# Attention and two mixture-of-experts layers in fp32: how the bias groups, the reciprocal sums and the V tails are handled in the attention part

## The chip, the core and the metric

The kernel runs on one core of one Trainium2 chip. The metric is the device time of one execution in microseconds (us). Before the change three runs gave 1418.03, 1415.32 and 1415.49 us, median 1415.49 us.

## The reference

Three stages follow each other; all arithmetic is fp32.

```python
def _attn_ref(q, k, v, w1, b1, w2):                 # B, H, S, D = 2, 8, 576, 64; 32 hidden values
    scores = 1.0 / np.sqrt(D) * np.matmul(q, k.transpose(0, 1, 3, 2))
    psi_rel = np.log1p(np.abs(pos[:, None] - pos[None, :]))
    psi_i = np.log1p(np.maximum(pos[:, None], 1.0))
    h = np.maximum((psi_rel / psi_i)[..., None] @ w1 + b1, 0.0)
    scores = scores + (h @ w2).transpose(2, 0, 1)[None]          # the bias, one map per head
    attn = np.exp(scores - np.max(scores, axis=-1, keepdims=True))
    return np.matmul(attn / (attn.sum(-1, keepdims=True) + 1e-09), v)
def _moe_ref(x, domain_probs, w1, w2):              # 1152 rows of 512, E = 4, F = 1024
    for e in range(E): out += p[:, e:e+1] * (np.maximum(x @ w1[e], 0.0) @ w2[e])
def _moe2_ref(x, w_gate, w1, w2):                   # E = 8; P from exp of logits, 8 Sinkhorn rounds
    for e in range(E): out += P[:, e:e+1] * (np.maximum(x @ w1[e], 0.0) @ w2[e])
```

## The kernel before, in words

The program is written in the order in which each engine works; nothing reorders it. `attention` comes first, `Moe.run` after it. TensorE is called PE here, VectorE DVE, ScalarE ACT, GpSimd POOL; SP issues all DMAs, in order.

**Bias.** The bias depends on the distance of two positions and on the row, so the kernel makes it in 36 groups of 16 rows. For a group four tiles of hidden values are made (`emit_hid`, L267: `tensor_scalar` on DVE or Relu on ACT), PE multiplies them with `w2` (`emit_bias_mm`, L278), ACT scales the product twice, forwards and reversed, into one of three staging rows (`emit_bias_out`, L298, two ACTIVATE at L313), and SP writes the row to DRAM (`bd`, L316). `load_bias` (L243) reads it back, shifted, as the tile `bt` that the scores need. Hidden values live in six places of `hids`; the product uses one bank `bps` where it has at most 512 columns, and otherwise one of the two `sc` buffers that the scores use. `groups(1)` emits one group, `hids(k)` makes k hidden tiles.

**Start.** The first FIRST = 8 groups are made at once (L476 to L491), with one `hids(2)` before and one after each, the first K and Q tiles being prepared between them (`prep_k`, `prep_q`). Then come the first two `load_bias`, which must wait for the eighth write. The other 28 groups are made inside the loop over units.

**Units.** A unit is a tile of 128 rows of queries for a pair of heads and one batch (in the four units of row tile 4, both batches with 64 rows each); there are 36, numbered 0 to 35 here, in the order row tile 0, 4, 1, 2, 3. Units 8 to 11 are row tile 4. Iteration k of the loop at L500 holds, in this order: scores of unit k (`emit_S`, PE L333), at its end on PE the tail of unit k-2 (`emit_tail`: one transpose, L379, and the two sums' reciprocals turned into rows by two 64-column matmuls with the identity, L382); the minimum of the negated scores with the bias added (`emit_max`, DVE L351, two instructions), the reciprocal of unit k-1's sums (L373, DVE); two exponentials on ACT (L364) with the copy of the first four transposed blocks between them (`emit_evac(k-2, 0)`); eight transposes of unit k-2 on PE (L396); one group (two in iterations 5, 8 and 12, with `hids(4)` between); the copy of the second four blocks on ACT; hidden tiles on DVE, with the copy of the tail's block (`emit_evac(k-2, 2)`, L403) on DVE after the first of them; the product with V of unit k-3 (`emit_P`, PE L423) and its scaling (`emit_x`, DVE L433). The tail's block stands in the second `sc` buffer of unit k, so the next unit's scores cannot start before it is copied out. Once all 36 groups are made (from iteration 25), the tail uses the bank `bps` and is copied by ACT, and the second four blocks by DVE.

In iterations 16 to 18 and from 23 on, one part of `piece` (L107 to L122, sums and fp32 splits of the finished rows for the next stage) stands at an iteration's end, a split with its high part on ACT (L99) and its low part on DVE or POOL (L100). From iteration 28 on the first weights are split too.

**V tails.** `load_v` (L196) puts the last 64 rows of V twice into the fifth block of `V`, in partitions 0 to 63 and 64 to 127, and `emit_P` multiplies the fifth block with 64 rows (L420 to L425): the first head in the lower, the second in the upper half.

**Mixture of experts.** From unit 35 on `Moe` takes over. None of its lines change.

## Time and profile before

| what | value |
|---|---|
| median of three runs | 1415.49 us |
| profiled execution, its own time | 1414.98 us |
| its span, first to last instruction | 1413.2 us |
| mean granted TensorE clock | 0.983 |
| PE busy | 1368.4 us (97%) |
| DVE busy | 812.8 us (58%) |
| ACT busy | 500.8 us (35%) |
| POOL busy | 376.1 us (27%) |

Some 1.8 us lie around the span. Attention takes about the first 235 us. The shares are averages over stages: in attention DVE and ACT are much busier than these shares say, and in the mixture of experts PE is. PE's busy time is modelled and says that matmuls are in flight, not that PE is at its peak. In a row of the timeline stand the start, the length, the engine, the line, the operation, the tiles written and read, the shape and the count; in brackets is the idle time of the engine before it and what ended it. "PEld" rows are weight loads, one before each matmul; "SPq" rows are DMA issues. "issue" means that the profile shows nothing that the engine waited for.

### The profile page before, as it was taken

The page shows a single profiled execution, that of the slowest core. Times are in us where ns is not written, and L with a number is a line of the kernel's source. Part 1 is how long each engine was busy: PE and PEld are TensorE (multiplying, and loading weights), DVE is VectorE, ACT ScalarE, POOL GpSimd, SP SyncE. Part 2 cuts the span into 40 slices and gives each one's busy share as a digit, 9 for nine tenths or more (in the row PEclk, how much of TensorE's full clock was granted, in tenths as well). Part 3 has the DMA queues.
Part 4 walks back from the last instruction along what each step waited for, and adds up shares of the span by engine and source line. Part 5 has one row for each costly group of instructions (what it writes and reads, how often), then busy time and mean ns, then how long its engine had stood idle before and what let it go on. Part 6 is the DMA issues. An engine that isn't in the chain of part 4 may idle for free.

```text
span 1413.2 us, 22618 instructions
## 1 busy us (share of the span) xinstructions
PE 1368.4 (97%) x8871; PEld 1177.3 (83%) x8871; DVE 812.8 (58%) x1810; ACT 500.8 (35%) x1184; POOL 376.1 (27%) x351
## 2 busy tenths in 40 slices
PE   6899999899999999999988999999999999999998
PEld 2566677789889898979877899899898898988987
DVE  5776887656355464385487464463553644735643
ACT  4666775324133142244232142241331422413311
POOL 0000122326044062054043062160440521603400
PEclk8899999999999999999999999999999999999999
DMA  6674531102011021011011021020120210200110
GB/s 176 183 181 121 147 104 61 60 30 90 1 60 61 1 90 31 0 55 65 1 60 61 1 83 38 8 89 24 34 87 1 66 54 1 90 31 31 61 38 31
DMA packets 41659, 84.95 MB, mean 60 GB/s; under 512 B 9296, under 2 KB 17232, under 8 KB 41552
## 3 DMA queue, kind: packets, MB, share of 16 engines
q1 hardware_dynamic: 41552, 83.50, 19.5%
q8 instruction: 70, 1.15, 0.3%
q14 instruction: 37, 0.30, 0.1%
HBM read 70.24 MB, written 13.25 MB: 59 GB/s over the span
## 4 chain that ended last, share of the span: by engine, by line
PE 89%; DVE 7%; ACT 2%; issue 1%; DMA 1%; SPq 0%; POOL 0%; DVEq 0%; ACTq 0%; POOLq 0%
PE y L714 41%; PE B L635 16%; PE C L635 10%; PE A L635 10%; PE po L423 3%; PE bps L287 2%; PE sc L333 2%; PE tp L396 2%; ACT s L364 1%; ACT bsts L313 1%; PE sc L382 1%; DVE s L351 1%; ACT at L405 0%; DVE wt L157 0%; PE sc L379 0%
## 5 line engine op out<-in xcount | busy, mean ns | idle before, releaser
L714 PE MATMUL y<-gb,h 128*128 128x512 f32 x2592 | 718.1, 397 | 0.0
L714 PEld LDWEIGHTS y<-gb,h 128*128 128x128 f32 x2592 | 454.4, 190 | 57.4 <-issue 0.2
L162 POOL TENSOR_TENSOR gb<-rawb,gb 128x512 fp32r<-128x512 f32 x94 | 126.3, 1356 | 640.7 <-ACT gb L161 637.0
L643 DVE TENSOR_TENSOR u<-B,s 128x320 f32<-128x320 f32 (+1 forms) x192 | 87.7, 457 | 306.9 <-PE B L635 306.9
L646 ACT ACTIVATE h<-c 128x320 fp32r<-128x320 f32 (+1 forms) x288 | 119.4, 439 | 400.3 <-DVE c L643 399.2
L649 DVE SCALAR_TENSOR_TENSOR h<-c,h 128x320 fp32r<-128x320 f32 (+1 forms) x288 | 169.5, 605 | 48.8 <-ACT h L646 44.0
L643 DVE TENSOR_TENSOR c<-C,u 128x320 f32<-128x320 f32 (+1 forms) x192 | 87.6, 456 | 61.4 <-PE C L635 57.9
L162 POOL TENSOR_TENSOR ga<-rawa,ga 128x512 fp32r<-128x512 f32 x94 | 120.8, 1304 | 4.5 <-ACT ga L161 4.5
L162 POOL TENSOR_TENSOR ga<-wt,ga 128x512 fp32r<-128x512 f32 x94 | 105.3, 1140 | 45.8 <-ACT ga L161 27.4
L657 ACT ACTIVATE s<-A 128x320 f32<-128x320 f32 (+1 forms) x96 | 39.5, 411 | 177.9 <-PE A L635 177.8
L646 ACT ACTIVATE h<-A 128x320 fp32r<-128x320 f32 (+1 forms) x96 | 39.1, 407 | 151.2 <-PE A L635 151.2
L643 DVE TENSOR_TENSOR c<-B,s 128x320 f32<-128x320 f32 (+1 forms) x96 | 43.9, 458 | 81.7 <-PE B L635 80.3
L161 ACT ACTIVATE gb<-rawb 128x512 fp32r<-128x512 f32 x96 | 60.0, 627 | 71.4 <-DMA rawb<-in_w 71.4
L364 ACT ACTIVATE s<-s,stat 128x576 f32<-128x576 f32 x72 | 55.5, 770 | 59.9 <-DVE stat L351 59.9
L635 PE MATMUL A<-x20A,ga 128*128 128x320 f32 x384 | 66.7, 309 | 0.0
L635 PE MATMUL C<-x20S,ga 128*128 128x320 f32 x384 | 66.6, 309 | 0.0
L635 PE MATMUL B<-x20S,ga 128*128 128x320 f32 x384 | 66.5, 308 | 0.0
L635 PEld LDWEIGHTS B<-x20S,ga 128*128 128x128 f32 x384 | 61.4, 188 | 5.7
L635 PEld LDWEIGHTS A<-x20A,ga 128*128 128x128 f32 x384 | 61.4, 188 | 5.6
L635 PEld LDWEIGHTS C<-x20S,ga 128*128 128x128 f32 x384 | 61.3, 188 | 5.7
L351 DVE CUSTOM_DVE_ANT_0 s<-sc,bt 128x576 f32<-128x576 f32 x72 | 51.7, 753 | 15.9 <-DMA bt<-bd 6.4
L287 PE MATMUL bps<-hids,w2n 128*32 128x288 f32 (+17 forms) x352 | 42.1, 523 | 18.6 <-DVE stat L351 8.1
(157 smaller groups left out, 1910.9 us busy)
## 6 DMA issues: line engine op xcount, KB each, us to landing
rawa<-in_w SPq DMA_DIRECT2D x48, 512.0 KB, 4.0
rawb<-in_w SPq DMA_DIRECT2D x48, 512.0 KB, 4.8
bd<-bsts SPq DMA_DIRECT2D x36, 295.5 KB, 3.3
bt<-bd SPq DMA_DIRECT2D x16, 512.0 KB, 4.3
qr<-in_qT SPq DMA_DIRECT2D x40, 64.0 KB, 3.0
kr<-in_kT SPq DMA_DIRECT2D x16, 144.0 KB, 3.2
V<-in_vT SPq DMA_DIRECT2D x4, 512.0 KB, 4.5
bt<-bd SPq DMA_DIRECT2D x8, 256.0 KB, 4.3
```

Of the source, the lines that this page charges most:

```text
L161: sc.activation(out=z(0), in_=src, func=AF.Copy)
L162: lo.tensor_tensor(out=z(1), in0=src, in1=z(0).bitcast(F32), op=ALU.subtract)
L287: pe.matmul(out=o[32 * q:32 * q + 32, j, 0:n], lhsT=w2n, rhs=hid[g, q][:, n * j:n * j + n], start=True, stop=True,)
L351: ve.tensor_tensor_reduce(out=s.rearrange("p (a j) -> p a j", a=2), in0=scps.pop((u, h))[:, :, 0:288], in1=bt[t, p][:, S * h:S * h + S].re ...
L364: sc.activation(out=s, in_=s, func=AF.Exp, scale=-1.0, bias=stat[u][:, h:h + 1], accum_out=stat[u][:, 2 + h:3 + h],)
L423: pe.matmul(out=o[64 * h:64 * h + 64, c0:c0 + n], lhsT=V[p][r, j, col:col + D], rhs=rhs, start=j == 0, stop=j == 4,)
L635: pe.matmul(out=ban[o], lhsT=a, rhs=x[:, z, k, :], start=not more and i == 0, stop=i == 5, skip_group_check=more,)
L643: ve.tensor_tensor(out=t[o], in0=ban[a], in1=t[b], op=ALU.add)
L646: sc.activation(out=h[f][:, 0, half, :], in_=src, func=AF.Relu)
L649: ve.scalar_tensor_tensor(out=h[f][:, 1, half, :], in0=src, scalar=0.0, in1=h[f][:, 0, half, :].bitcast(F32), op0=ALU.max, op1=ALU.subtract,)
L657: sc.activation(out=t["s1"], in_=ban["A"], func=AF.Copy)
L714: pe.matmul(out=self.y[t], lhsT=a, rhs=x, start=g == 0 and f == 0 and i == 0, stop=g == NP - 1 and f == 1 and i == 2,)
```

## The change

1. `load_v` clears the fifth block of V on POOL (`memset`) and then loads, for each head, only that head's columns into its half of the partitions. The fifth product now has 128 rows like the others; the foreign half is multiplied by zeros.
2. `emit_recip2` spreads the two reciprocals of a row over a 128x128 tile `spread` (POOL copy from a broadcast source), and `emit_tail` transposes that tile in one 128-column transpose where two matmuls stood.
3. The copy of the tail's block (`emit_evac(k-2, 2)`) is always on ACT, between the second exponential and the group's scaling.
4. `emit_x` of unit k-4 stands right after `emit_max(k)`; before, that of unit k-3 stood after `emit_P(k-3)`.
5. The first eight groups are made with twelve places for hidden tiles (six more in three tiles of `xa`; `load_k` now turns over four of these tiles, not seven) and three PSUM buffers for the product, hidden tiles are made two groups ahead, and three more groups stand after the first `load_bias`. Iterations 5, 8 and 12 have one group like the others.

```diff
         def load_v(p):
             sy.dma_start(out=V[p][:, 0:4, :], in_=vT[p, 0:512].rearrange("(j p) x -> p j x", p=128))
+            gp.memset(V[p][:, 4, :], 0.0)
             for h in range(2):
-                sy.dma_start(out=V[p][64 * h:64 * h + 64, 4, :], in_=vT[p, 512:576])
+                to, of = (x.rearrange("p (b h d) -> p h b d", b=2, h=2)[:, h] for x in (V[p][:, 4, :], vT[p, 512:576]))
+                sy.dma_start(out=to[64 * h:64 * h + 64], in_=of)
...
+        free = [(i, hids_[:, i * S:i * S + S]) for i in range(6)]
+        taken = {}
+        MORE = 56
...
+            if started == 6:
+                for i in XA[4:]:
+                    x = xa.tile([128, 1280], F32, tag=f"x0{i}", name=f"hid{i}")
+                    free.extend([(6, x[:, 0:S]), (6, x[:, S:2 * S])])
...
-            if nb == 1:
+            if nb == 1 and (made >= FIRST or made % 3 == 1):
                 o = pt.tile([128, 1, 512], F32, tag="bps", name=f"bps{g}", bufs=1)
...
-            ve.reciprocal(stat[u][:, 6:8], stat[u][:, 4:6])
+            st = stat.pop(u)
+            ve.reciprocal(st[:, 6:8], st[:, 4:6])
+            spread[u] = atb.tile([128, 128], F32, tag="spread", name=f"spread{u}", bufs=2)
+            gp.tensor_copy(
+                spread[u].rearrange("p (h d) -> p h d", h=2), st[:, 6:8].unsqueeze(2).to_broadcast([128, 2, D])
+            )
...
             pe.transpose(o[:, 1, :], s[:, 512:640], ident)
-            st = stat.pop(u)
-            for h in range(2):
-                pe.matmul(
-                    out=o[64 * h:64 * h + 64, 0, :], lhsT=st[:, 6 + h:7 + h].to_broadcast([128, 64]),
-                    rhs=ident, start=True, stop=True,
-                )
+            pe.transpose(o[:, 0, :], spread.pop(u), ident)
...
-                        rhs = a[h][:, j, i0:i0 + n] if j < 4 else a[2][r, 1, i0:i0 + n]
+                        rhs = a[h][:, j, i0:i0 + n] if j < 4 else a[2][:, 1, i0:i0 + n]
...
-                            lhsT=V[p][r, j, col:col + D],
+                            lhsT=V[p][:, j, col:col + D],
...
-        hids(4, (1,))
+        hids(8, (1, 5))
         for g in range(FIRST):
-            hids(2, (1,))
             groups(1)
...
+            hids(4, (1,))
...
         load_bias(*tps_[0])
         load_bias(*tps_[1])
         load_k(*kq[5])
+        load_q(*tps_[3])
+        prep_q(*tps_[1])
         prep_k(*kq[2], sc)
-        load_q(*tps_[3])
+        for _ in range(3):
+            groups(1)
+            hids(4)
         prep_k(*kq[3], sc)
...
                     emit_recip2(k - 1)
+                if k >= 4:
+                    emit_x(k - 4)
...
-            late = made == NGR
-            if late and k - 2 < U:
+            if k >= 2 and k - 2 < U:
                 emit_evac(k - 2, 2, sc)
-            ng = 2 if k in (5, 8, 12) else 1
-            for i in range(ng):
-                groups(1)
-                if i < ng - 1:
-                    hids(4)
+            groups(1)
```

The order on ACT in iteration 5 before: `s` are the exponentials, `at` the copies of transposed blocks, `bsts` the scaling of a group (two rows each).

```order
L364 ACTIVATE s_631,stat_630<-s_631,stat_630 128x576
L405 ACTIVATE at_646<-tp_636 128x512
L364 ACTIVATE s_631,stat_630<-s_631,stat_630 128x576
L313 ACTIVATE bsts<-bps_649,cst 128x432
L313 ACTIVATE bsts<-bps_649,cst 128x160
L313 ACTIVATE bsts<-bps_661,cst 128x416
L313 ACTIVATE bsts<-bps_661,cst 128x176
L405 ACTIVATE at_669<-tp_641 128x512
```

The same iteration on ACT in the changed kernel.

```order
L377 ACTIVATE s_678,stat_677<-s_678,stat_677 128x576
L418 ACTIVATE at_696<-tp_686 128x512
L377 ACTIVATE s_678,stat_677<-s_678,stat_677 128x576
L418 ACTIVATE at_699<-sc_662 128x256
L326 ACTIVATE bsts<-bps_701,cst 128x384
L326 ACTIVATE bsts<-bps_701,cst 128x208
L418 ACTIVATE at_709<-tp_691 128x512
```

The copy out of `sc` has come in ahead of the group, and the second group is gone.

DVE between the first eight groups and the minimum of unit 0 (L351) before: the last hidden tiles, then the low parts of two K tiles (`kk`).

```order
L273 TENSOR_SCALAR hids<-T,b1psi 128x464 x3
L273 TENSOR_SCALAR hids<-T,b1psi 128x528 x3
L225 TENSOR_TENSOR kk_289<-kr_137,kk_289 128x576
L225 TENSOR_TENSOR kk_295<-kr_215,kk_295 128x576
L351 ISA s_313,stat_312<-sc_298,bt_280 128x576
```

The same stretch of DVE in the changed kernel (`hidS` are the places in `xa`).

```order
L283 TENSOR_SCALAR hids<-T,b1psi 128x544 x3
L241 CAST qq_296<-qr_134 128x256
L242 TENSOR_TENSOR qq_296<-qr_134,qq_296 128x256
L227 TENSOR_TENSOR kk_299<-kr_137,kk_299 128x576
L283 TENSOR_SCALAR hids<-T,b1psi 128x560 x2
L283 TENSOR_SCALAR hidS_149<-T,b1psi 128x560 x2
L283 TENSOR_SCALAR hidS_150<-T,b1psi 128x576 x2
L283 TENSOR_SCALAR hidS_151<-T,b1psi 128x576 x2
L283 TENSOR_SCALAR hids<-T,b1psi 128x448 x4
L227 TENSOR_TENSOR kk_350<-kr_224,kk_350 128x576
L364 ISA s_368,stat_367<-sc_353,bt_284 128x576
```

Twelve hidden tiles now stand between the first `load_bias` and the first minimum; before, there were none behind the eighth group but the three of the ninth.

PE in iteration 5 behind the scores before (`sc`: the tail, `tp`: the transposes).

```order
L379 MATMUL sc_614<-kept,s_484 128x128
L382 MATMUL sc_614<-kept,stat_483 64x128 x2
L396 MATMUL tp_636<-kept,s_484 128x128 x4
L396 MATMUL tp_641<-kept,s_484 128x128 x4
L287 MATMUL bps_649<-hids,w2n 32x432 x4
L287 MATMUL bps_661<-hids,w2n 32x416 x4
```

The same in the changed kernel.

```order
L397 MATMUL sc_662<-kept,s_535 128x128
L398 MATMUL sc_662<-kept,spread_607 128x128
L409 MATMUL tp_686<-kept,s_535 128x128 x4
L409 MATMUL tp_691<-kept,s_535 128x128 x4
L297 MATMUL bps_701<-hids,w2n 32x384 x4
```

Ten transposes of one shape now follow each other, and one group follows them.

## Rows read from the trace of the kernel before

**Rows 1.** Timeline, DVE: first minimum of units 0, 4, 8, 14, 25 and 35

```profile
33.78 0.76 DVE L351 CUSTOM_DVE_ANT_0 s<-sc,bt 128x576 f32<-128x576 f32 x1 [5.17 <-DMA bt<-bd]
...
57.65 0.75 DVE L351 CUSTOM_DVE_ANT_0 s<-sc,bt 128x576 f32<-128x576 f32 x1
...
79.76 0.76 DVE L351 CUSTOM_DVE_ANT_0 s<-sc,bt 128x576 f32<-128x576 f32 x1 [1.54 <-DMA V<-in_vT]
...
120.01 0.76 DVE L351 CUSTOM_DVE_ANT_0 s<-sc,bt 128x576 f32<-128x576 f32 x1 [0.78 <-PE sc L333]
...
175.40 0.75 DVE L351 CUSTOM_DVE_ANT_0 s<-sc,bt 128x576 f32<-128x576 f32 x1
...
217.75 0.75 DVE L351 CUSTOM_DVE_ANT_0 s<-sc,bt 128x576 f32<-128x576 f32 x1
```

**Rows 2.** Timeline, PE's weight loads in unit 16, to the next unit's scores

```profile
128.73 0.82 PEld L333 LDWEIGHTS sc<-kk,qq 64*128 64x128 f32 x12 [0.17 <-issue]
...
129.72 0.14 PEld L379 LDWEIGHTS sc<-kept,s 128*128 128x128 f32 x1 [0.17 <-issue]
...
130.35 0.85 PEld L396 LDWEIGHTS tp<-kept,s 128*128 128x128 f32 x8 [0.17 <-issue]
...
132.15 0.85 PEld L423 LDWEIGHTS po<-at,V 128*64 128x64 f32 x16 [0.63 <-DVE at L403]
...
133.18 0.19 PEld L423 LDWEIGHTS po<-at,V 64*64 64x64 f32 x4 [0.17 <-issue]
...
133.54 0.82 PEld L333 LDWEIGHTS sc<-kk,qq 64*128 64x128 f32 x12 [0.17 <-issue]
```

**Rows 3.** Timeline, DVE and ACT in unit 16

```profile
129.92 0.76 DVE L351 CUSTOM_DVE_ANT_0 s<-sc,bt 128x576 f32<-128x576 f32 x1 [0.78 <-PE sc L333]
...
130.78 0.78 ACT L364 ACTIVATE s<-s,stat 128x576 f32<-128x576 f32 x1 [1.23 <-DVE stat L351]
...
131.69 0.42 DVE L403 COPY at<-sc 128x256 f32<-128x256 f32 x1
...
132.04 0.77 ACT L364 ACTIVATE s<-s,stat 128x576 f32<-128x576 f32 x1
...
132.80 1.03 ACT L313 ACTIVATE bsts<-bps,cst 128x208 f32<-128x208 f32 x2
```

**Rows 4.** Second group of unit 12 in the timeline; busy time and granted clock after it

```profile
108.44 0.75 PE L287 MATMUL bps<-hids,w2n 128*32 128x320 f32 x8 [2.36 <-ACT bsts L313]
...
109.10:116.00 6.90, 6.90 (x67) 5.58 (x64) 3.45 (x12) 2.41 (x6) 0.00 (x0) 0.51 0.42 109
```

**Rows 5.** Timeline: minimum of unit 9, last bias load for unit 11, its minimum

```profile
87.82 0.76 DVE L351 CUSTOM_DVE_ANT_0 s<-sc,bt 128x576 f32<-128x576 f32 x1
...
95.64 0.60 SPq L254 DMA_DIRECT2D bt<-bd  x1
...
99.40 0.76 DVE L351 CUSTOM_DVE_ANT_0 s<-sc,bt 128x576 f32<-128x576 f32 x1 [1.47 <-PE sc L382]
```

**Rows 6.** Timeline: bias writes, a group's work on ACT and DVE, first eight groups

```profile
8.85 6.90 SPq L316 DMA_DIRECT2D bd<-bsts  x4
...
15.13 2.42 DVE L273 TENSOR_SCALAR hids<-T,b1psi 128x512 f32<-128x512 f32 x6
...
17.14 1.05 ACT L313 ACTIVATE bsts<-bps,cst 128x512 f32<-128x512 f32 x2 [1.34 <-PE bps L287]
...
18.09 0.68 ACT L275 ACTIVATE hids<-T,b1psi 128x480 f32<-128x480 f32 x1
...
23.73 3.41 SPq L316 DMA_DIRECT2D bd<-bsts  x2
```

**Rows 7.** Timeline: a DVE sum alone, and the same beside a POOL instruction

```profile
174.99 0.29 DVE L115 TENSOR_TENSOR rows<-rows,t 128x128 f32<-128x128 f32 x1
...
187.43 0.46 POOL L100 TENSOR_TENSOR x10A<-rows,x10A 128x128 fp32r<-128x128 f32 x1 [0.45 <-ACT x10A L99]
187.50 0.52 DVE L115 TENSOR_TENSOR rows<-rows,t 128x128 f32<-128x128 f32 x1
```

More of the change, by code (lines that the diff above doesn't have):

```diff
@@ L211, in load_k @@
             i = 2 * p + b
-            r = xa.tile([128, 1280], F32, tag=f"x0{XA[i % 7]}", name=f"kr{p}{b}")[:, 0:S]
+            r = xa.tile([128, 1280], F32, tag=f"x0{XA[i % 4]}", name=f"kr{p}{b}")[:, 0:S]
             for h in range(2):
@@ L265, in ranges @@
             return fwd, rev, n, 1 if n <= 512 else 2
+        free = [(i, hids_[:, i * S:i * S + S]) for i in range(6)]
+        taken = {}
+        MORE = 56
         def emit_hid(g, eng, q):
             tt = 4 * g + q
-            i = started % 6 * S
-            x = hids_[:, i:i + S]
+            if started == 6:
+                for i in XA[4:]:
+                    x = xa.tile([128, 1280], F32, tag=f"x0{i}", name=f"hid{i}")
+                    free.extend([(6, x[:, 0:S]), (6, x[:, S:2 * S])])
+            place = free.pop(0)
+            taken[g, q], x = place, place[1]
             n = ranges(g)[2]
@@ L295, in emit_bias_mm @@
                 hid.pop((g, q))
+                place = taken.pop((g, q))
+                if place[0] < 6 or started < MORE:
+                    free.append(place)
             return o
@@ L321, in attention @@
         scps, sm, at_t, po, rc = {}, {}, {}, {}, {}
-        stat = {}
+        stat, spread = {}, {}
         def emit_S(u):
@@ L419, in emit_P @@
                     for h in range(2):
-                        r = slice(0, 128) if j < 4 else slice(64 * h, 64 * h + 64)
                         col = (2 * bb + h) * D
-                        rhs = a[h][:, j, i0:i0 + n] if j < 4 else a[2][r, 1, i0:i0 + n]
+                        rhs = a[h][:, j, i0:i0 + n] if j < 4 else a[2][:, 1, i0:i0 + n]
                         pe.matmul(
                             out=o[64 * h:64 * h + 64, c0:c0 + n],
-                            lhsT=V[p][r, j, col:col + D],
+                            lhsT=V[p][:, j, col:col + D],
                             rhs=rhs,
@@ L463, in hids @@
             for i in range(k):
-                if started < 4 * NGR:
+                if started < 4 * NGR and (free or started == 6):
                     emit_hid(order[started // 4], sc if i in engs else ve, started % 4)
@@ L476, in attention @@
         FIRST = 8
-        hids(4, (1,))
+        hids(8, (1, 5))
         for g in range(FIRST):
-            hids(2, (1,))
             groups(1)
+            if g == 0:
+                prep_q(*tps_[0])
             if g == 1:
-                prep_q(*tps_[0])
                 prep_k(*kq[0], ve)
+            hids(4, (1,))
             if g == 3:
                 load_k(*kq[3])
+            if g == 4:
                 prep_k(*kq[1], ve)
-                prep_q(*tps_[1])
-            if g == 5:
+            if g == 6:
                 load_k(*kq[4])
                 load_q(*tps_[2])
-            hids(2)
         load_bias(*tps_[0])
@@ L510, in attention @@
                     emit_recip2(k - 1)
+                if k >= 4:
+                    emit_x(k - 4)
             elif k == U:
                 emit_recip2(k - 1)
+                emit_x(k - 4)
                 st_sc.close()
@@ L525, in attention @@
                 emit_exp(k, 1)
-            late = made == NGR
-            if late and k - 2 < U:
+            if k >= 2 and k - 2 < U:
                 emit_evac(k - 2, 2, sc)
-            ng = 2 if k in (5, 8, 12) else 1
-            for i in range(ng):
-                groups(1)
-                if i < ng - 1:
-                    hids(4)
+            groups(1)
             if k >= 2 and k - 2 < U:
                 emit_evac(k - 2, 1, sc if made < NGR else ve)
-            hids(1)
-            if k >= 2 and k - 2 < U:
-                if not late:
-                    emit_evac(k - 2, 2, ve)
-            hids(1)
+            hids(2)
             if k < U:
@@ L545, in attention @@
                 emit_P(k - 3)
-                emit_x(k - 3)
+                if k >= U:
+                    emit_x(k - 3)
             if first:
```

## Prediction, made before the changed kernel ran

> **What bounds the kernel now.** I read the start times of the first minimum of chosen units, because every unit passes through that instruction on DVE [rows 1]. They cut the attention part into five stretches: 33.78 us to unit 0, 23.87 to unit 4, 22.11 to unit 8, 40.25 to unit 14, 55.39 to unit 25, and 42.35 to unit 35. What comes after, the mixture of experts, is not touched, and only its start can move.
>
> Then the weight loads of a unit on PE, late in the middle stretch [rows 2]. Unit 16's scores start at 128.73, the next unit's at 133.54: 4.81 us, and between the loads stand only pauses of 0.17 us, always where the tile's form changes, and the time in which the group's matmuls run (the 0.63). So PE sets the pace there. The tail costs 129.72 to 130.35, 0.63 us, for one transpose and two 64-column products, while eight transposes of the same shape take 0.85, or 0.106 each.
>
> Then DVE and ACT of the same unit [rows 3]. The minimum starts 1.19 us after the scores do, the first exponential 0.86 after that, the second 1.26 after the first, and the group's scaling 0.76 later, at 132.80, with 1.03 of work. DVE's copy of the tail's block, which frees the `sc` buffer, started at 131.69, long before the next scores at 133.54. It is not on the path now.
>
> Last, the places with a second group. In iteration 12 PE waits 2.36 us for its one bank until ACT has scaled the first group; behind that wait PE's granted clock is 0.51 for 6.90 us, that is at 1.2 GHz almost throughout, though PE was busy all the time [rows 4].
>
> **The change part by part.** The sum is made against the profiled execution, 1414.98 us; the median of the runs, 1415.49, is 0.5 above it.
>
> *Start.* Eight groups now end when the last bias write is issued: the two writes from 23.73 take 3.41 [rows 6], an issue itself 0.60 [rows 5], so the eighth goes at 26.5; the first went at 8.85 [rows 6]. That is 2.5 us a group. ACT's own work for a group is 1.05 of scaling and 0.68 for one hidden tile, 1.73 us [rows 6]. With twelve places and three PSUM buffers nothing else should hold a group: 8.85 + 7 x 1.73 = 21.0. The K and Q loads queued ahead of the eighth write on SP are moved by nothing and can cost up to one us, so I take 21.9. Everything from that write to the first minimum (26.5 to 33.78, 7.3 us) stays: first minimum at 29.2, **-4.6 us**. Under this cover lie the three groups: on ACT 3 x 1.05, on DVE 12 hidden tiles at 0.40 (six took 2.42 [rows 6]), 4.8 us. They fit into the 7.3 with the preparation of K and Q, but barely. If they don't, the first minimum is late by what sticks out, up to the three groups' own 4.8.
>
> *Units 0 to 3.* Group 8 to 10 no longer share the `sc` buffers with these units, but the K casts stay between ACT and DVE. Nothing gained leaves 23.87; the pace of unit 16 for all four would be 19.2. I take 22.8, near the upper end since those casts stay in order behind the group's scaling: **-1.1**.
>
> *Steady pace.* On PE the second transpose costs 0.106, and one change of form goes: the tail's 0.63 becomes 0.21 (two transposes in the run of ten), -0.42. The V tail in the form of the other four blocks saves one pause of 0.17 and costs nothing, since its four loads take 0.19, as four of the others do (0.85/16 each) [rows 2]. PE's 4.81 becomes 4.22. But the copy of the tail's block now comes after the second exponential on ACT: from scores to that copy's end 1.19 + 0.86 + 1.26 + 0.76, and some 0.4 for the copy itself (0.42 on DVE [rows 3]), then the next scores. That ring is 4.5 us, longer than PE's 4.22. **ACT's queue takes over from PE**, and the pace is 4.5, not 4.22. In row tile 4 the scores are twice as many (about 0.8 more): 5.3.
>
> *Units 4 to 8.* Three at 4.5 and one at 5.3 make 18.8 against 22.11, mostly the second group of iteration 5: **-3.3**.
>
> *Units 8 to 14.* Two second groups and the slow clock lie here [rows 4]. But bias tiles arrive by SP: unit 11's minimum started at 99.40, 3.2 after the issue of its last load at 95.64 had ended, and 11.58 after unit 9's minimum, which is the reader that frees the buffer [rows 5]. SP's queue holds that unit's bias write first (which waits for the group's scaling), then Q, then four loads. Nothing in the change shortens it; the scaling comes 0.27 later behind the moved copy, so two units cost 11.85. Unit 8 to 9 at 5.3, 9 to 11 at 11.85, then three units at about 4.8 (four 64-row products remain in them): 31.5 against 40.25, **-8.7**.
>
> *Units 14 to 25.* Six units have no split part; 4.8 to 5.0 becomes 4.5: -2.6. In the five others DVE's last low part waits for ACT's high part behind exponentials, group and copies, which the change does not shorten, and slack that PE's lateness used to absorb is gone: I give back half. **-1.3**; the bounds are 0 and 11 x 0.59 = -6.5.
>
> *Units 25 to 35.* No groups any more; the same DVE and ACT queue holds split parts in every unit. I take **0**, bounds 0 and -6.5. Moving `emit_x` forward saves DVE a wait there that the split parts use up.
>
> *After unit 35* PE does three more tails and four more V products without pause, -1.9 at most; DVE's weight splits hold half of it: **-1.0**.
>
> *New on POOL and SP.* 36 spread copies: the nearest row is a 128x128 POOL sum of 0.46 [rows 7]. The copy starts after the reciprocal, over 2 us before PE's tail asks for it, so its length is hidden; four memsets hold back only V's tails on SP, which are needed units later. But a DVE sum beside such a POOL instruction took 0.52 instead of 0.29 [rows 7], so each copy may cost DVE some 0.23. DVE has that much to spare in the 4.5; I count nothing, and at most 36 x 0.23 = 8 us. The Trainium skill ("SBUF — State Buffer", Who interferes with whom) says that GpSimd and VectorE share one port pair under an exclusive lock, the loser blocked for the whole instruction. By it up to 0.46 per unit would be lost, 16 us; the row shows half of that for a late overlap.
>
> Sum: -4.6 - 1.1 - 3.3 - 8.7 - 1.3 - 0 - 1.0 = -20.0, **1395.0 us**.
>
> **The rivals.**
> *PE stays the bound.* If the moved copy's ring is shorter than I think, units 14 to 35 gain what PE gains, 0.59 each. For it: PE was busy without a gap there [rows 2]. Against it: the sum of the ring. It would add some 11 us: 1384.
> *The cover is too short.* The three groups stick out of the round trip (+4.8), and ACT's longer ring eats the 2.6 of units 14 to 25 and the 1.0 at the end: 1395 + 8.4, some 1404. For it: the three groups barely fit.
> *DVE blocked by the spread copies, so slower.* Place: DVE's queue behind the reciprocal in every unit. With 20 us gained elsewhere it decides from 20/36 = 0.56 us per copy, if every copy is long and lies on the path; at 0.7 it is 1395 + 25 = 1420. For it: rows 7 show the interference. The skill's lock is this mechanism. Against it: 0.46 is the nearest length.
> *The groups gain nothing.* If the reads of the bias or the K casts set every start and PE's savings are all absorbed, only noise is left: 1415.
>
> **How the numbers follow.** Forecast (1390 to 1400) 0.58, PE stays the bound 0.15, cover too short 0.20, blocked DVE 0.04, nothing gained 0.03. The likeliest case gives 1395.0. The range takes in the forecast, the short cover up to 1405, and of the PE case its slower part, down to 1385. About 0.2%, or 2.8 us, is what a measurement of this kernel can tell from no change; so faster 0.93, within 0.2% 0.03, slower 0.04.
>
> **What would show it.** First minimum near 29 and unit 4's near 52, unit 14's near 102, unit 25's near 156, unit 35's near 198. In units 19 to 22 scores start every 4.5 us, and PE has short waits before them that ACT's copy of `sc` ends. No second group's wait on PE and no slow clock around unit 12. DVE's hidden tiles stay at their length beside the spread copy. Wrong: a first minimum after 31 (the cover), a pace of 4.2 (PE bound), a pace above 4.8 with DVE late (POOL), or bias tiles arriving earlier than 11 us after the buffer's reader.

## The result, and the profile after

Four runs of the changed kernel took 1395.53, 1398.83, 1400.68 and 1400.79 us, median 1399.76; the kernel before took 1415.72 beside them (median of four). The ratio is 0.9878, with a 95% interval from 0.9854 to 0.9902: faster by 1.2%. The forecast was 1395.0 us, with a range from 1385 to 1405. By the medians 16.0 us are gained. The trace is that of the fastest of the four, 1395.53 us; its span is 1393.6 against 1413.2, 19.6 less. The other three have no trace, so where they take their 3 to 5 us more is not shown. PE is busy 1343.9 us (96%), DVE 802.7, ACT 506.7, POOL 389.3.

The first minima of units 0, 4, 8, 14, 25 and 35 in the timeline of DVE:

```profile
28.99 0.76 DVE L364 CUSTOM_DVE_ANT_0 s<-sc,bt 128x576 f32<-128x576 f32 x1 [1.21 <-DMA bt<-bd]
...
53.03 0.75 DVE L364 CUSTOM_DVE_ANT_0 s<-sc,bt 128x576 f32<-128x576 f32 x1
...
71.03 0.76 DVE L364 CUSTOM_DVE_ANT_0 s<-sc,bt 128x576 f32<-128x576 f32 x1 [1.76 <-PE sc L346]
...
103.32 0.76 DVE L364 CUSTOM_DVE_ANT_0 s<-sc,bt 128x576 f32<-128x576 f32 x1 [0.96 <-PE sc L346]
...
155.51 0.74 DVE L364 CUSTOM_DVE_ANT_0 s<-sc,bt 128x576 f32<-128x576 f32 x1
...
198.23 0.76 DVE L364 CUSTOM_DVE_ANT_0 s<-sc,bt 128x576 f32<-128x576 f32 x1
```

Set against [rows 1], unit 35 comes 19.5 us earlier, and the span is 19.6 shorter: all of the gain in this trace is made before unit 35. By stretch it is 4.8 us to unit 0, -0.2 from 0 to 4, 4.1 from 4 to 8, 8.0 from 8 to 14, 3.2 from 14 to 25 and -0.4 from 25 to 35.

PE's weight loads in unit 21 of the changed kernel, a plain unit (with a group, without split parts), and the group's matmuls that run in the 0.76 us where no weights are loaded. Behind them stand the scores' loads of units 21 and 22 in the kernel before:

```profile
135.79 0.83 PEld L346 LDWEIGHTS sc<-kk,qq 64*128 64x128 f32 x12 [0.17 <-issue]
136.78 0.14 PEld L397 LDWEIGHTS sc<-kept,s 128*128 128x128 f32 x1 [0.16 <-issue]
136.83 0.14 PEld L398 LDWEIGHTS sc<-kept,spread 128*128 128x128 f32 x1
136.94 0.91 PEld L409 LDWEIGHTS tp<-kept,s 128*128 128x128 f32 x8
138.02 0.16 PEld L297 LDWEIGHTS bps<-hids,w2n 128*32 128x32 f32 x8 [0.17 <-issue]
138.93 1.07 PEld L435 LDWEIGHTS po<-at,V 128*64 128x64 f32 x20 [0.76 <-DVE rows L445]
140.18 0.83 PEld L346 LDWEIGHTS sc<-kk,qq 64*128 64x128 f32 x12 [0.17 <-issue]
```
```profile
138.02 0.99 PE L297 MATMUL bps<-hids,w2n 128*32 128x464 f32 x8
```
```profile
153.52 0.82 PEld L333 LDWEIGHTS sc<-kk,qq 64*128 64x128 f32 x12 [0.17 <-issue]
...
158.46 0.82 PEld L333 LDWEIGHTS sc<-kk,qq 64*128 64x128 f32 x12 [0.17 <-issue]
```

The rows answer to [rows 2]. The tail is two loads that run on into the eight transposes (136.78 to 136.94, 0.16 us), and the V products are one run of twenty loads with no pause inside. Scores start 4.39 us apart. Nothing but pauses of 0.17 and the group's own matmuls lies between, so **PE still sets the pace here**: the same distance was 4.94 before, and the difference of 0.55 is nearly the whole 0.59 that the two edits were to save on PE.

Around iteration 0 there are waits that the kernel before did not have. SP's queue, ACT and PE in the changed kernel (three cuts of its timeline; the first row is the eighth bias write):

```profile
21.59 0.54 SPq L329 DMA_DIRECT2D bd<-bsts  x1
24.90 0.39 SPq L255 DMA_DIRECT2D bt<-bd  x1
...
26.36 0.47 SPq L256 DMA_DIRECT2D bt<-bd  x1
26.92 1.14 SPq L216 DMA_DIRECT2D kr<-in_kT  x2
28.10 1.24 SPq L232 DMA_DIRECT2D qr<-in_qT  x2
29.44 5.97 SPq L329 DMA_DIRECT2D bd<-bsts  x4
```
```profile
33.82 1.05 ACT L326 ACTIVATE bsts<-bps,cst 128x16 f32<-128x16 f32 x2 [2.40 <-DMA bd<-bsts]
```
```profile
34.92 1.80 PE L346 MATMUL sc<-kk,qq 64*128 64x288 f32 x11 [2.43 <-ACT bsts L326]
```

The bias writes of the three early groups stand in SP's queue behind two bias loads, a K load and a Q load, and go from 29.44 on. Until the first of them has landed there is no free staging row, so the scaling of iteration 0's group waits 2.40 us, and PE, whose scores need the `sc` buffer of that group, waits 2.43. Unit 0 to 1 takes 7.54 us instead of 5.64.

In row tile 4 (units 8 to 11) and at unit 12, DVE waits for bias tiles:

```profile
83.08 0.76 DVE L364 CUSTOM_DVE_ANT_0 s<-sc,bt 128x576 f32<-128x576 f32 x1 [2.70 <-DMA bt<-bd]
...
88.50 0.76 DVE L364 CUSTOM_DVE_ANT_0 s<-sc,bt 128x576 f32<-128x576 f32 x1 [1.76 <-DMA bt<-bd]
...
94.70 0.76 DVE L364 CUSTOM_DVE_ANT_0 s<-sc,bt 128x576 f32<-128x576 f32 x1 [2.51 <-DMA bt<-bd]
```

Where [rows 4] had a clock of 0.51, the changed kernel has full speed in the same units; the longest stretch of its low clock, 1.2 GHz, lies in the first iterations, where PE had waited for the bias (windows: stretch, length, busy time of PE, PEld, DVE, ACT and POOL, granted clock, DMA share, GB/s):

```profile
94.70:103.30 8.60, 6.91 (x127) 5.63 (x123) 6.75 (x22) 7.21 (x18) 1.28 (x4) 1.00 0.58 155
28.90:39.10 10.20, 6.86 (x42) 3.33 (x44) 6.82 (x20) 4.99 (x12) 1.42 (x4) 0.50 0.72 205
```

### The profile page after: what moved, and what is told of

Same layout as the page of the kernel before. It is cut to its first block, busy times and chain, and to the rows that moved or that the text cites. A ratio compares the mean times of both kernels' runs of the same rounds, so it can differ in the third digit from the quotient of the medians.

```text
span 1393.6 us, 22438 instructions
## 1 busy us (share of the span) xinstructions
PE 1343.9 (96%) x8763; PEld 1171.4 (84%) x8763; DVE 802.7 (58%) x1786; ACT 506.7 (36%) x1208; POOL 389.3 (28%) x391
## 4 chain that ended last, share of the span: by engine, by line
PE 83%; DVE 9%; ACT 3%; DMA 2%; issue 1%; SPq 1%; DVEq 0%; ACTq 0%
PE y L726 41%; PE B L647 16%; PE C L647 10%; PE A L647 10%; DVE s L364 2%; PE po L435 2%; PE sc L346 1%; ACT s L377 1%; DMA bt<-bd 1%; PE bps L297 1%; PE tp L409 1%; ACT bsts L326 1%; DMA bd<-bsts 1%; DVE wt L157 0%; ACT at L418 0%
## 5 line engine op out<-in xcount | busy, mean ns | idle before, releaser
L661 DVE SCALAR_TENSOR_TENSOR h<-c,h 128x320 fp32r<-128x320 f32 (+1 forms) x288 | 165.7, 592 | 49.1 <-ACT h L658 43.8
L435 PEld LDWEIGHTS po<-at,V 128*64 128x64 f32 x800 | 39.4, 137 | 33.9 <-DVE rows L445 32.0
L435 PE MATMUL po<-at,V 128*64 128x128 f32 (+1 forms) x800 | 47.7, 267 | 15.6 <-DVE rows L445 15.4
```

The lines of the kernel that those rows point to most:

```text
L435: pe.matmul(out=o[64 * h:64 * h + 64, c0:c0 + n], lhsT=V[p][:, j, col:col + D], rhs=rhs, start=j == 0, stop=j == 4,)
L661: ve.scalar_tensor_tensor(out=h[f][:, 1, half, :], in0=src, scalar=0.0, in1=h[f][:, 0, half, :].bitcast(F32), op0=ALU.max, op1=ALU.subtract,)
```

## The experiments

Theory 1 is that of the prediction: the bias part carries nearly all of the gain (fast start, no second groups), and the time saved on PE by the other edits mostly vanishes in rings through ACT, DVE and SP (a ring is a loop of waits from engine to engine that closes once per unit, so that its sum is the least a unit can take). Theory 2 is that the saved PE time carries it. The measured ratios are to the kernel before on the same chip. Since the clock makes runs differ by a few us, each run is also read by the first minima in its trace, which repeat closely: the changed kernel's second trace is 1.15 us later at unit 0 and agrees with the first within 0.15 us in each stretch after that. Unit 0 to 1 scatters more: 7.09 to 7.71 us in the runs whose edits do not reach it. That a unit "takes" so long means the time from the first minimum of the unit before it to its own. In us:

```
                              unit 0   0-4    4-8    8-14   14-25  25-35   0 to 35
before                         33.78  23.88  22.11  40.25  55.39  42.35   183.98
changed                        28.99  24.04  18.00  32.29  52.19  42.72   169.24
changed, again                 30.14  24.13  18.01  32.15  52.16  42.72   169.17
second groups back             29.70  23.39  21.08  38.95  52.27  42.73   178.42
before + bias part             29.34  23.93  18.73  31.72  55.82  42.35   172.55
two 64-column products         29.45  23.77  19.08  32.16  55.11  42.76   172.88
V tails of 64 rows             29.84  24.55  18.32  33.01  53.21  43.61   172.70
tail's copy on DVE             30.02  23.65  17.68  31.34  51.49  42.69   166.85
output product last            29.52  23.98  18.04  33.94  52.53  41.01   169.50
output product first           29.70  23.97  18.02  32.16  53.31  42.40   169.86
bias loads early               29.49  23.60  18.00  28.85  52.21  42.72   165.38
bias writes early              29.32  22.89  18.01  34.33  52.17  42.72   170.12
three edits combined           29.44  22.10  17.68  28.17  51.48  42.70   162.13
and output product last        29.49  22.40  17.47  28.08  51.45  40.98   160.38
```

**The changed kernel again.** No edit.

> The changed kernel itself once more, beside the next three on one chip. Both theories: the ratio of the first measurement, 0.9878, within 0.003; the first minima of all units within 0.7 us of the first trace, up to the first one's start; what differs between runs should be the number of 3.4 us slices with a low clock after unit 35, each worth some 1.7 us.

Ratio 0.9888 (0.9867 to 0.9909), 1397.08 us (1395.79 to 1399.24). Against the expectation, unit 0 came 1.15 us later than in the first trace; the distances repeat. It is the measure for the runs below.

**Second groups back.**

```diff
-        for _ in range(3):
-            groups(1)
-            hids(4)
...
-            groups(1)
+            for i in range(2 if k in (5, 8, 12) else 1):
+                groups(1)
+                hids(4 * (k in (5, 8, 12) and i == 0))
```

> The changed kernel, but the three groups of the first round trip go back to second groups in iterations 5, 8 and 12; places, buffers and the other parts stay as changed. Theory 1 (the bias carries the gain: fast start, no second groups): the start keeps its 4.6 us, the stretches 4 to 8 and 8 to 14 lose the 4.1 and 8.0 us that they gained, and the first minimum comes up to 2 us earlier since three groups no longer lie in the round trip. So 1399.8 + 12.1 - 2 = 1410 us, between 1407 and 1413, with a clock near 1.2 GHz around iteration 12 again. Theory 2 (the saved TensorE time carries the gain, 36 x 0.59 = 21 us, and the second groups were hidden): no more than 3 us slower, below 1403.

Ratio 0.9956 (0.9942 to 0.9970): 10 to 11 us of the gain are gone, 9.3 by the trace from unit 0 to 35. Units 5 to 6, 8 to 9 and 12 to 13 take 7.40, 8.10 and 8.85 us, where the changed kernel takes 4.37, 5.71 and 4.26: 10.0 us at three places. This is the cause, in iteration 12 of this run (timeline, PE):

```profile
99.95 0.72 PE L297 MATMUL bps<-hids,w2n 128*32 128x304 f32 x8
...
104.23 1.27 PE L297 MATMUL bps<-hids,w2n 128*32 128x320 f32 x8 [3.56 <-ACT bsts L326]
```

The second group waits 3.56 us for the one bank, as in [rows 4], and then takes 1.27 us where the first took 0.72. Unit 0 to 1 is back at 5.59: the early groups do cost 2 us there. They cost unit 0 nothing (29.70 without them, 28.99 to 30.14 in the runs with them).

**Before, with the bias part alone.** Twelve places for hidden values, K buffers on four tiles, three buffers for the products at the start, no second groups. All else as before. The core of it:

```diff
-            i = started % 6 * S
-            x = hids_[:, i:i + S]
+            place = free.pop(0)
+            taken[g, q], x = place, place[1]
...
-            if nb == 1:
+            if nb == 1 and (made >= FIRST or made % 3 == 1):
...
+        for _ in range(3):
+            groups(1)
+            hids(4)
...
-            ng = 2 if k in (5, 8, 12) else 1
-            for i in range(ng):
-                groups(1)
-                if i < ng - 1:
-                    hids(4)
+            groups(1)
```

> The kernel before with the bias part of the change alone (twelve places, three buffers at the start, three groups in the round trip, no second groups); reciprocals by two 64-column products, 64-row V tails, DVE's tail copy and the product of the outputs as before. Theory 1: it keeps nearly all of the gain, 4.8 us of the start, 4.1 and 8.0 us of units 4 to 14 minus about 10 x 0.3 that the faster units had there: 1415.7 - 14 = 1402 us, between 1399 and 1405. Theory 2: it gains no more than 5 us: above 1410.

Ratio 0.9899 (0.9884 to 0.9914), 1399.79 us where before took 1413.67: -13.9 us by the medians, as theory 1 expected. In its trace unit 35 comes 15.9 us earlier than before, in the two of the changed kernel 19.5 and 18.5. Which of the start's parts (places, buffers, tiles made two groups ahead) makes the start fast was not tried. All other edits together add 3.4 us up to unit 35 (172.55 against 169.17). The next four runs take them apart.

**Two 64-column products.** The reciprocals go as two matmuls, POOL makes no spread copy.

```diff
...
-            pe.transpose(o[:, 0, :], spread.pop(u), ident)
+            for h in range(2):
+                pe.matmul(out=o[64 * h:64 * h + 64, 0, :], rhs=ident, start=True, stop=True,
+                          lhsT=st[:, 6 + h:7 + h].to_broadcast([128, 64]))
```

> The changed kernel with two 64-column products in the place of the transpose of the spread reciprocals; GpSimd makes no spread copy, VectorE's reciprocal stays where it is. TensorE's tail costs 0.42 us more per unit. Theory 1 (a ring through ScalarE's copy of 4.3 to 4.5 us and the bias tiles set the pace, TensorE is close behind with 4.22): TensorE goes to 4.64 and becomes the bound in some 11 units without other waits, +0.3 each, so +2 to +5 us: 1402 to 1405. Theory 2 (every saved TensorE time counts): 36 x 0.42 = 15 us slower, 1415. A third way, if the spread copies block VectorE: no loss or a gain, below 1399.

Ratio 0.9912 (0.9895 to 0.9929), 1400.39 us: on this chip the changed kernel's two ratios give 1396.4 and 1397.8, so 2.6 to 4.0 us slower. The size is that of theory 1, its reason is not. Units 21 to 24 take 4.88, 4.79, 4.83 and 4.84 against 4.48, 4.39, 4.41 and 4.44: the whole 0.4 in each plain unit, as it must be where PE was the bound already; with another ring ahead of PE a part of it would be hidden. The third way is out: without spread copies nothing gets faster.

**V tails of 64 rows.**

```diff
-            gp.memset(V[p][:, 4, :], 0.0)
...
+                        r = slice(0, 128) if j < 4 else slice(64 * h, 64 * h + 64)
...
-                            lhsT=V[p][:, j, col:col + D],
+                            lhsT=V[p][r, j, col:col + D],
```

> The changed kernel with the 64-row V tails of before, without zeroed rows. Theory 1 (each saved pause of TensorE counts only in units that TensorE bounds): TensorE's 4.22 becomes 4.39, while the other rings stand at 4.1 to 4.5, so less than half of 36 x 0.17 = 6 us is lost: 0 to 2.5 us slower than the changed kernel (ratio up to 0.0018 higher). Rival (TensorE bounds all units): 6 us slower. The other way (the row padding costs TensorE more than the pause): 1 us or more faster.

Ratio 0.9907 (0.9889 to 0.9924), 1401.49 us, again some 3 us slower than the changed kernel; by the trace 3.5 (172.70 against 169.17), between the two theories. Units 21 to 24 lose 0.14 to 0.16 each, and the late units 26, 27, 29, 32, 33 and 35 the same 0.15. The pause lies on the path there as well.

**Tail's copy on DVE.** While groups are made, the block of the tail is copied by DVE behind one hidden tile, as before.

```diff
-            if k >= 2 and k - 2 < U:
+            late = made == NGR
+            if late and k >= 2 and k - 2 < U:
                 emit_evac(k - 2, 2, sc)
...
-            hids(2)
+            hids(1)
+            if not late and k >= 2 and k - 2 < U:
+                emit_evac(k - 2, 2, ve)
+            hids(1)
```

> The changed kernel with the copy of the tail's block on VectorE behind one hidden tile, as before, while groups are made (iterations 2 to 24); afterwards on ScalarE as in both. Theory 1 (ScalarE's copy closes the ring that sets 4.3 to 4.4 us in the plain units): the ring goes, TensorE's own 4.22 remains, so 0.1 to 0.2 us in some 10 units, 1 to 2 us faster: 1397 to 1400. Rival (VectorE's queue is fuller, the copy comes late there, and the move to ScalarE was needed): 20 units by 0.2 to 0.4, 4 to 8 us slower: 1404 to 1408.

Ratio 0.9860 (0.9845 to 0.9875), 1394.53 us; the interval overlaps that of the changed kernel, so the time alone is unclear. The trace is not: 2.3 us shorter from unit 0 to 35. But not where theory 1 had it. Units 21 to 24 take 17.69 us together against 17.72: no ring through the copy sets the plain units. The gain is in units 0 to 4 (0.5), where ACT also casts K, in 8 to 14 (0.8), and in the units with split parts. ACT in the changed kernel, unit 16, behind the second exponential, shows what lies in a row:

```profile
114.80 0.37 ACT L418 ACTIVATE at<-sc 128x256 f32<-128x256 f32 x1
115.07 1.04 ACT L326 ACTIVATE bsts<-bps,cst 128x208 f32<-128x208 f32 x2
116.01 0.59 ACT L418 ACTIVATE at<-tp 128x512 f32<-128x512 f32 x1
116.48 0.31 ACT L99 ACTIVATE x10A<-rows 128x128 fp32r<-128x128 f32 x1
```

The moved copy lengthens this queue by its 0.27 to 0.37, and the casts of K and the high parts that stand behind it come that much later: units 17 to 18 and 18 to 19 take 5.87 and 5.50 with it, 5.58 and 5.22 without.

**Output product last.** `emit_x(k - 3)` stands behind `emit_P(k - 3)` again in every iteration, as before the change.

```diff
-                if k >= 4:
-                    emit_x(k - 4)
...
                 emit_P(k - 3)
-                if k >= U:
-                    emit_x(k - 3)
+                emit_x(k - 3)
```

> The changed kernel with the product of the outputs as before: unit k-3's, at the end of iteration k, behind its V products. Theory 1: VectorE then waits at each iteration's end for TensorE's V products before it may take the next minimum's place or the next splits; the plain units 14 to 25 get 0.1 to 0.2 slower (1 to 2 us), while units 20 and 33 take 3.34 again (1.5 us); together within 1 us of the changed kernel. Rival (the early product closes the late units' ring of 4.10 and costs): units 25 to 35 go 1 us and more faster than 42.7, and the whole by as much. Other rival (the early product is what frees VectorE): 3 us or more slower.

Ratio 0.9860 (0.9840 to 0.9880); this interval overlaps too. Units 25 to 35 take 41.01 us instead of 42.72, the gain that the first rival expected: 27 takes 3.61 (4.10) and 33 takes 2.94 (4.10). The waits of PE's weight loads in the changed kernel, from 156 us to 199 (us in total, times, longest):

```profile
PEld po L435 <- DVE rows L445: 10.6, 10, 1.7
```

and one such unit in its timeline:

```profile
162.61 0.83 PEld L346 LDWEIGHTS sc<-kk,qq 64*128 64x128 f32 x12 [0.17 <-issue]
...
163.77 0.90 PEld L409 LDWEIGHTS tp<-kept,s 128*128 128x128 f32 x8
165.47 1.07 PEld L435 LDWEIGHTS po<-at,V 128*64 128x64 f32 x20 [0.79 <-DVE rows L445]
166.71 0.82 PEld L346 LDWEIGHTS sc<-kk,qq 64*128 64x128 f32 x12 [0.17 <-issue]
```

No group fills the gap here: the V products wait 0.79 us for the previous unit's product on DVE, which now stands behind the minimum. That closes a ring, scores, minimum, reciprocal, product, V products, next scores, of 4.10 us. It costs where nothing else is as long: units 27 and 33 make up nearly the whole gain, and the other eight stay within 0.04 us. The move costs at the hand-over too: the first weight load of the mixture of experts comes 3.00 us behind unit 35's first minimum in the changed kernel, 1.69 in this run. From unit 0 to 35 this trace is still no shorter (169.50 against 169.17), mainly because it lost 1.5 us in unit 14 (5.90 against 4.37), where a new stretch of low clock fell:

```profile
100.20:103.60 3.40, 3.40 (x33) 2.00 (x33) 1.74 (x8) 3.06 (x8) 0.50 (x2) 0.50 0.51 130
```

Why it fell there is not shown; the fastest version below has the product at the same place and no such stretch.

**Output product first.** The product of unit k-4 stands ahead of the minimum of unit k.

```diff
                 emit_S(k)
+                if k >= 4:
+                    emit_x(k - 4)
                 emit_max(k)
                 if k > 0:
                     emit_recip2(k - 1)
-                if k >= 4:
-                    emit_x(k - 4)
```

> The changed kernel with the product of unit k-4's outputs ahead of unit k's minimum on VectorE, instead of behind it and the reciprocal. Theory 1 (in the late units a ring scores, minimum, reciprocal, product, V products, next scores takes 4.10 us, since the V products of unit k-3 wait for that product): the wait goes, the units that took 3.34 before the change take it again, about 0.75 each in unit 20 and unit 33 and perhaps two more, so 1.5 to 3 us faster than the changed kernel. Rival (VectorE's queue sets those units anyway, and the product ahead of the minimum delays it by its 0.3): nothing, or up to 3 us slower.

Ratio 0.9889 (0.9865 to 0.9912): no difference, as the rival had it. Unit 33 takes 2.94, but most other late units take 0.18 to 0.24 more: the product of 0.27 us now stands ahead of the minimum. The place that works is the old one.

**Bias loads early.**

```diff
                 emit_max(k)
+                if (t == 4 or b == 1) and ti + 2 < len(tps_):
+                    load_bias(*tps_[ti + 2])
...
-            if k < U and last and ti + 2 < len(tps_):
-                load_bias(*tps_[ti + 2])
```

> The changed kernel with a row tile's bias loads written right behind the minimum that frees their buffer, ahead of the iteration's bias write and Q load in SP's queue. Theory 1 (units 10, 11 and 12 wait 2.70, 1.76 and 2.51 us for bias tiles because SP's queue stands behind a bias write that waits for ScalarE): the loads end 2 us and more earlier, the three units go at TensorE's 5.3 and the stretch 8 to 14 takes 2 to 3.5 us less. Rival (the buffer's reader and the landing alone set it, or the bias writes behind the loads come late and hold a staging row): less than 0.7 us gained.

Ratio 0.9852 (0.9829 to 0.9874), 1392.09 us; all its runs (up to 1393.06) lie below all of the changed kernel beside it (from 1395.79). Units 8 to 14 take 28.85 instead of 32.15: 3.3 us, within the 2 to 3.5 expected. First minima of units 11 and 12 in this run (timeline, DVE), against 88.50 and 94.70 above:

```profile
87.00 0.76 DVE L364 CUSTOM_DVE_ANT_0 s<-sc,bt 128x576 f32<-128x576 f32 x1 [1.40 <-PE sc L346]
...
91.30 0.76 DVE L364 CUSTOM_DVE_ANT_0 s<-sc,bt 128x576 f32<-128x576 f32 x1 [0.36 <-PE sc L346]
```

They wait for PE now. The bias loads were late because of what stood ahead of them in SP's queue.

**Bias writes early.** The K and the Q load go behind the three groups.

```diff
-        load_k(*kq[5])
-        load_q(*tps_[3])
         prep_q(*tps_[1])
         prep_k(*kq[2], sc)
         for _ in range(3):
             groups(1)
             hids(4)
+        load_k(*kq[5])
+        load_q(*tps_[3])
```

> The changed kernel with the K load and the Q load of the round trip written behind its three groups, so that their bias writes stand directly behind the two bias loads in SP's queue. Theory 1 (iteration 0's scaling waits 2.40 us for a staging row because these writes stand behind those loads): the wait shrinks to 1.2 us or less, unit 0 to 1 takes 5.7 to 6.5 instead of 7.54, and 1 to 1.8 us are gained. Rival (the K casts on ScalarE set units 1 to 4, and the later K load makes the next one wait): unit 4 comes where it came, within 0.4 us of 53.0, and nothing is gained.

Ratio 0.9898 (0.9877 to 0.9919): nothing gained in all. Up to unit 4 theory 1 holds (timeline, ACT; the wait was 2.40):

```profile
33.08 1.05 ACT L326 ACTIVATE bsts<-bps,cst 128x16 f32<-128x16 f32 x2 [1.33 <-DMA bd<-bsts]
```

Unit 0 to 1 takes 6.48, and 0 to 4 22.89 instead of 24.13: 1.2 us, of which some 0.6 is beyond the scatter of unit 0 to 1. Unit 12 then comes 0.8 us later behind its predecessor (6.71 against 5.95), and units 12 to 14 take 1.6 us more (10.20 against 8.62), of which 3.40 us run at 1.2 GHz:

```profile
97.70:101.10 3.40, 3.40 (x20) 3.12 (x20) 2.14 (x7) 2.27 (x6) 0.02 (x1) 0.50 0.39 99
```

The waits for bias tiles in units 10 to 12 lie just before it; but the changed kernel has such waits and no such stretch, and with the output product last one fell at 100.20 without the early writes. So the cause stays open. The combined version below, which has the early writes and not those waits, has no such stretch.

**Three edits combined.** Tail's copy on DVE, bias loads early, bias writes early.

> The changed kernel with three edits together: the copy of the tail's block on VectorE while groups are made, the bias loads right behind the minimum, the K and Q loads of the round trip behind its three groups. Theory 1: the gains lie in different stretches and add: 2.4 (units 0 to 25, tail copy) + 3.4 (units 8 to 13, bias loads) + 1.2 (units 0 to 1, writes) = 7 us faster than the changed kernel, 1390 beside 1397, ratio 0.983 to 0.985. Rival (what made the early writes alone slower, the clock falling once more near 98 us, is there too): no better than the bias loads alone, 1392, ratio 0.985 and more.

Ratio 0.9817 (0.9797 to 0.9838), 1389.06 us. From unit 0 to 35 it takes 162.13 us, 7.0 less than the changed kernel: the gains add.

**And output product last.** The same, with `emit_x(k - 3)` behind `emit_P(k - 3)`.

> The three edits of the combined version and, as a fourth, the product of the outputs at the iteration's end again, behind its V products, as before the change. Theory 1 (the early product closes a ring in the late units, 4.10 where 3.34 to 3.61 are possible, and the early clock loss of that run near 100 us came from the waits for bias tiles, which are gone here): units 25 to 35 take 41 instead of 42.7, 1.2 to 2 us faster than the combined version: ratio 0.980 to 0.981. Rival (with the tail's copy on VectorE its queue now waits for the V products and holds that copy and the next minimum): units 14 to 25 lose what units 25 to 35 gain, ratio 0.9817 or more.

Ratio 0.9780 (0.9761 to 0.9799), 1383.03 us, **the fastest version**: 32 us below the kernel before, and, by the ratios 0.9780 and 0.9878, 14 us below the changed kernel. Units 25 to 35 take 40.98, and units 14 to 25 lose nothing (51.45 against 51.48). By the medians it gains 6 us on the combined version, more than the 1.7 of the late units. In the two traces 1.3 us of the rest lie at the hand-over (1.69 against 3.00 us, as above), and 2.5 at the start of the first mixture of experts (the first 224 weight loads of its hidden layer take 71.8 us against 74.3); why these come from this edit was not tried.

## Why the prediction was right, and where its reasons were not

*Start, -4.6: right, by its own steps.* The eighth write goes at 21.59 where 21.9 was forecast, and the first minimum stands 7.4 us behind it where 7.3 was taken. That is -4.8 in the first trace; later traces lie 0.3 to 1.2 us behind it. The three groups fit under the round trip, as the run without them shows. The rival of the short cover fails at unit 0, but not altogether, see the next point.

*Units 0 to 3, -1.1: wrong,* +0.2. The step counted the three groups' work on ACT and DVE and forgot their DMAs: three bias writes in SP's queue behind four bias loads, K and Q, and only three staging rows. Early writes alone gave 0.6 to 1.2 us of it back. The moved copy, ahead of the K casts, took another 0.5.

*Steady pace, "ACT's queue takes over from PE" and 4.5: wrong.* The plain units go at 4.3 to 4.4, which is PE's own time: the 4.22 was read in unit 16, and the group's matmuls, for which no weights are loaded during 0.63 us there, take 0.76 in unit 21. The ring through the moved copy was mis-sized at 4.5. In unit 16 the copy ends at 115.17 (114.80 and 0.37 in ACT's rows above), and PE's scores go from there:

```profile
110.83 0.91 PEld L346 LDWEIGHTS sc<-kk,qq 64*128 64x128 f32 x12 [0.17 <-issue]
...
115.17 0.87 PEld L346 LDWEIGHTS sc<-kk,qq 64*128 64x128 f32 x12 [0.17 <-issue]
```

That is a ring of 4.34. With the copy on DVE the same distance is 4.26 (110.00 to 114.26), and units 21 to 24, where PE itself needs more, take what they took. So in plain units the first rival, PE stays the bound, was the right mechanism, and both PE edits count nearly in full: 0.4 and 0.15 a unit.

*Units 4 to 8, -3.3, and 8 to 14, -8.7: right* (-4.1 and -8.0). The second groups are 10.0 us of the gain. The bias ring was forecast at 11.85 for two units; units 8 to 10 took 12.05 and 9 to 11 11.75 (first minima). The row of [rows 5] from which it was read names PE's tail, not the bias tile, as what ended that wait, so before the change the ring was at most as long as PE's work there. In the changed kernel the waits end with the bias tile, and the early loads confirm the cause.

*Units 14 to 25, -1.3: the total was too small (-3.2), and its parts were mis-sized.* Of the plain units' 0.59 some 0.55 came through. Against that stands what units 18 to 20 lose: 5.86, 5.50 and 4.26, where before took 5.59, 5.22 and 3.40. The moved copy explains the first two. The 3.40 comes back only with copy and product both undone (3.42 in the fastest version).

*Units 25 to 35, 0: the number was right (+0.4), the reason was not.* The V tails gain 0.9 here and the early product costs 1.7. The prediction gave that move credit for a freed DVE and did not look at who waits for the product: the next unit's V products, though they write another part of the tile `po`.

*After unit 35, -1.0:* the time from unit 35's first minimum to the end of the span is 1195.4 us in both traces, so nothing was gained there. Over all traces this time lies between 1191.2 and 1199.5, so that a gain of 1 us could not be told from scatter.

*Spread copies: right to count nothing in the sum, though they do touch DVE.* POOL's copies in the changed kernel (ns, minimum, median, longest; first and last start):

```profile
L389 POOL COPY spread<-stat x36: 289/290/546, 38.1 to 201.8; 128x128 f32<-128x128 f32 x36
```

At a median of 0.29 us they are far from the 0.56 from which the rival decides, and they gain what two products cost. In twelve late units a copy runs beside DVE's copy out of `tp`, which takes 0.68 us with it and 0.69 in the run without spread copies. But where a copy meets a hidden tile over its whole length, the tile takes longer than others of its shape, by 0.09 to 0.13 us in seven such tiles. This one has 448 columns (timeline, DVE and POOL; the third row is from the run without spread copies, with the mean in ns behind the busy time):

```profile
129.76 0.57 DVE L283 TENSOR_SCALAR hids<-T,b1psi 128x448 f32<-128x448 f32 x1
129.79 0.29 POOL L389 COPY spread<-stat 128x128 f32<-128x128 f32 x1 [3.62 <-DVE stat L387]
L283 DVE TENSOR_SCALAR hids<-T,b1psi 128x448 f32<-128x448 f32 x3 | 1.2, 445 | 0.0
```

The Trainium skill ("SBUF — State Buffer", Who interferes with whom) says that of a VectorE instruction in a 2-port mode and a GpSimd instruction the one that issues first has the shared ports for its whole length, while the other is fully blocked. If the tile runs in such a mode, which no row shows, this trace does not agree: the copy starts 0.03 us behind the tile and still takes 0.29, and it is the tile that takes some 0.12 more. In these seven tiles that is less than 1 us of DVE's time in all.

In all, undoing one edit at a time, from unit 0 to 35: the early groups gained 9.3 us, the spread transpose 3.7 and the V tails 3.5; the moved copy cost 2.3, and the moved product 1.7 in the late units. Counted so, the four smaller edits sum to 3.2, close to the 3.4 between the bias part alone and the whole; by its whole trace, with the lost clock in unit 14, undoing the moved product gained nothing.

Of the 19.6 us in the first trace 16.9 lie where the forecast had them and for its reasons: the start and units 4 to 14. The rest was forecast at -3.4 and measured -2.7, and that fit is luck: the forecast left out gains on PE of 7 us and losses of 4, and their net of some 3 happens to lie near what it had for other reasons.

## What to carry to other kernels

When an edit moves work into a wait, price its DMAs and buffers as well as its engine time, by their place in the one queue that issues them. Before counting a step as free because its engine has slack, list who waits for its result: a product moved ahead, behind a longer instruction, closed a new ring here. A forecast whose total fits can hold gains and losses that cancel; undoing the edits one by one finds the losses, and without these two, with two pieces of SP's queue put in another order, the kernel was 14 us faster still.

## What was not expected of the hardware

A gain in one place can be taken back by the clock in another: with the early writes some 1.2 us came off units 0 to 4, and a stretch of 3.40 us at a granted 0.50 then fell on units 13 and 14, where the changed kernel ran at full clock, and these took 1.6 more. Such stretches also came in two other versions, at 100.20 with the output product last and at 128.30 with it first, each in one trace, so that the early writes are the cause is not shown. The changed kernel's runs differ by 5 us at mean clocks between 0.985 and 0.989; this is about as much as one of its smaller edits is worth, so the stretches of a trace told these edits apart where the medians could not.

A POOL copy beside a DVE instruction lengthened it in part, and not always: a hidden tile that met a copy of 0.29 us took some 0.12 us more, a DVE copy out of `tp` took no more.
